# RWKV-7 attention with a hardswish FFN: b and k turned by VectorE from second loads by quarters, and the last features of y copied by GpSimd

## The chip, the cores and the metric

One core of a Trainium2 chip runs the whole kernel. Its engines work side by side, each through its own list of instructions in order: TensorE (PE in the profile) multiplies matrices and, by a multiplication with the identity, transposes them; VectorE (DVE), ScalarE (ACT) and GpSimd (POOL) work on elements; SyncE (SP) issues transfers here. PEld is PE's loading of the stationary operand. Semaphores tie the lists together. The metric is the device time of one execution in microseconds; lower is better. A comparison uses the median of several executions.

## The reference

There are 4 batches, 8 heads, 768 steps and a head dimension of 40, all in fp32. For each batch and head a state of 40x40 runs through the steps, and the output of a step is read before the state is updated:

```python
for t in range(S):
    y[:, :, t] = np.einsum('bhd,bhde->bhe', rt, state)
    Sa = np.einsum('bhde,bhe->bhd', state, at)
    state_decay = state * wt[:, :, None, :] - np.einsum('bhd,bhe->bhde', Sa, bt)
    state = state_decay + np.einsum('bhd,bhe->bhde', vt, kt)
```

The 8 x 40 = 320 outputs of a step are then one token of an FFN over 3072 tokens, 320 to 2048 to 320:

```python
h = x @ w_in
g = h * np.clip(h + 3.0, 0.0, 6.0) / 6.0
out = g @ w_out
```

## The kernel before

The recurrence is computed in blocks of 64 steps. A **unit** is one block of one pair of batches, so there are 24 units (0 to 23), and four units are a group (128 steps of all batches). Steps lie on the partitions in the loads; for the products, features have to lie there, so the inputs are transposed.

Work of a unit comes in named stages of two kinds. `prepare(i)` is ahead of the recurrence: W and gam (running products of the decay w: gam, and its inverse rgam), A, B, K (the inputs turned so that features lie on the partitions, and multiplied by gam or rgam: `at`, `bt`, `kt`), F and E (masked products of these), factor (rgam turned back, from which GpSimd makes KBt, k and b with steps on the partitions, L725) and EV (E times v, L752). `step(i)` goes with the recurrence: fade, RT, VT, R, C, S, U, UT, rS, H, ysn (the outputs y), then `move` and `move2`, which bring the 320 features of y from the tile `yg` into the layout that the FFN reads, `xt`, three pieces of 128, 128 and 64 features. The triangular systems of a group are solved together by `invert`, a chain of some sixty dependent VectorE operations (L804, L810) with copies around it.

The order of the instructions on each engine is written out in the code; no scheduler moves them. From unit 8 on `a_block(m)` emits the stages, a block at a time. A unit begins every three blocks from unit 8 to 12, and every four from unit 13 on. `together` issues the PE products of all stages of a block in the order of PRODUCTS, and then what reads their results in the order of RESULTS; products of a block share PSUM tiles of two banks (`pair`) where they fit. Between the blocks `feed` puts pieces of the FFN (`expand`, L1171 and `short`, L1184, the first product; L1193 and L1194 the activation; `contract`, L1219, the second product) and of the inversion. `short` takes the 64 last features; beside a product that uses only half of the array it goes in fours of 64x64.

How the inputs are turned: from unit 8 on, b is turned by `turn_halves` (L516, eight PE transposes into PSUM) and k by `turn_pairs` (L506, four PE transposes). a, and r from unit 4 on, are already turned by VectorE: `turn_blocks` (L524 to L531) uses VectorE's transpose of 32x32 blocks, and for this the tile has to be loaded by quarters (`fetch`, L478: four transfers, 32 partitions each, of 80 or 48 features a head pair). A tile that is loaded so holds the values in an order that only this transpose reads; GpSimd's KBt needs b and k as they come in the plain loads (L490, two transfers).

SP issues all of this: loads, `xt` moves (`move`, L1111, four transfers; `move2`, L1116, four more of 32 features x 128 tokens each), outputs (L1243) and the weights' pieces at the start (L343). It is one queue in order: a transfer whose tile is still in use holds back all that stand behind it. `fetch` for the next unit is called in the stage that has read the tile: a's in A, b's and k's in factor behind KBt, v's in K (that of the unit itself). The weights arrive as eight pieces of w_in and those of w_out in the first 150 us, and ScalarE and VectorE convert each (L393 to L403, a factor; the raw pieces lie in tiles that are used for something else later). FEATURES says which features of the model go on which partitions of which of the three pieces, and so how w_in is loaded: two transfers a piece.

The tiles `xt` come from a ring of six, which also lends places to the first sums of the FFN (`part`, L1228).

Of the kernel before, what the change touches and what calls it, by code (L numbers as in the profile page):

```python
# [17 lines left out]
P = 128  # L18
BL = 64
HB = BL // 2  # L20
L = 32
# [10 lines left out]
def kernel(  # L32
# [179 lines left out]
    area = const.tile([P, EDGE + 3 * H * BL], F32, name="area")  # L212
# [30 lines left out]
    tinv = const.tile([P, NH, BL], F32, name="tinv")  # L243


    state, last_dec = [], []
    for p in range(NP):
# [12 lines left out]
        [(0, 0, 2 * D), (2 * D, 4 * D, D + 8)],  # L260
        [(0, 2 * D, 2 * D), (2 * D, 6 * D, D + 8)],
        [(0, 5 * D + 8, L), (L, 7 * D + 8, L)],
# [188 lines left out]
    def fetch(name, i, engine=None):  # L451

        if i is None or i >= NK:
            return
        x, crossed = {"W": (w, 0), "A": (a, 0), "B": (b, 0), "K": (k, 0), "R": (r, 1),
                      "V": (v, 1)}[name]
        if name == "V":
            t = values[i % AHEAD]
        else:
            t = placed.get((name, i))  # L460
            if (name, i) == ("R", 1):
                t = others["K"]
            if (name, i) == ("W", NU + 1):
                t = values[NU]
            t = t if t is not None else (others if i < 2 * NU and i % 2 and name != "R" else inputs)[name]
        g, p = names[i]
        engines = engine or nc.sync
        if name == "R" and i >= NU or name == "A" and i >= 2 * NU:
            y = x[2 * p:2 * p + 2, :, g * BL:(g + 1) * BL, :]
            n = 2 if name == "R" else 1  # L470
            y = y.rearrange("q (k s j) t e -> s j (q k) (t e)", s=2, j=n).rearrange(
                "s j k (l e) -> s j l k e", e=2 * D)
            for s in range(2):
                for c in range(0, D, L):
                    z = s * SLOT + c
                    to = rooms[name][z:z + L].rearrange("l (j k e) -> l j k e", j=n, e=2 * D)
                    for j in range(n):
                        nc.sync.dma_start(out=to[:, j, :, 0:2 * D - c], in_=y[s, j, :, :, c:])  # L478
            data[i][name + "N"] = t
            return  # L480
        for q in range(2):
            engine = engines[q] if isinstance(engines, tuple) else engines
            y = x[2 * p + q, :, g * BL:(g + 1) * BL, :]
            rows = slice(q * BL, (q + 1) * BL)
            if crossed:
                for s in range(2):
                    engine.dma_start(out=t[rows, 4 * s:4 * s + 4, 0:D],
                                     in_=y[s::2].rearrange("h t e -> t h e"))
            else:
                engine.dma_start(out=t[rows, :, 0:D], in_=y.rearrange("h t e -> t h e"))  # L490
        data[i][name + "N"] = t
# [32 lines left out]
    def turn_blocks(to, name):  # L524

        x = rooms[name].rearrange("p (j k y e) -> p j k y e", j=2, y=2, e=D)[:, :, :, :, 0:L]
        if name == "A":
            nc.vector.transpose(out=to[:].rearrange("p r (q t y) -> p q r y t", q=2, y=2), in_=x)
            return
# [32 lines left out]
    def begun_beside():  # L562

        begin = -(-(SCAN + 1) // 16) * 16
        for n, name in enumerate("KB"):
            x = area[:, begin + n * H * JOIN:begin + (n + 1) * H * JOIN]
            nc.gpsimd.memset(x, 0.0)
            beside[name] = x.rearrange("p (h t) -> p h t", h=H)
        beside["E"] = grp.tile([P, H, BL], F32, name="E", tag="U", bufs=1)
        nc.gpsimd.memset(beside["E"][:], 0.0)  # L570
        for name in "rgam", "RT":
# [10 lines left out]
    def prepare(i, F):  # L582
        n, o = i % NU, data[i]
        halves = i >= 2 * NU
# [68 lines left out]
        def b_stage():  # L653
            x = turn_in(o["BN"], halves)
            yield PE
            bt = o["bt"] = turned("bt")
            for y, z, g in zip(parts_of(bt, halves), x, parts_of(o["rg"], halves)):
# [74 lines left out]
        def k_stage():  # L732
            x = turn_pairs(o["KN"])
            yield PE
            kt = o["kt"] = turned("kt")
            nc.vector.tensor_tensor(out=kt[:], in0=x[:], in1=o["rg"][:], op=ALU.mult)
# [24 lines left out]
        return {"W": w_stage, "gam": gam_stage, "A": a_stage, "B": b_stage, "F": f_by_32 if i < 2 * NU else f_by_64,  # L761
# [121 lines left out]
    def step(i):  # L883
# [216 lines left out]
        def s_move():  # L1100
            xt = m["xt"] = ffn.tile([P, 3, P], F32, name="xt", bufs=6)
            yg = m["yg"]
            moves = m["moves"] = [(xt[0:D, 0:2], yg[0:D, 0:2, :]),
                     (xt[D:2 * D, 0:2], yg[SLOT:SLOT + D, 0:2, :]),
                     (xt[2 * D:3 * D, 0:2], yg[0:D, 2:4, :]),
                     (xt[3 * D:P, 0:2], yg[SLOT:SLOT + 8, 2:4, :])]
            for c in range(4):
                moves.append((xt[c * L:(c + 1) * L, 2],
                              yg[SLOT + 8:SLOT + D, 2 + c % 2, :]))
            for dst, src in moves[:4]:  # L1110
# [3 lines left out]
        def s_move2():  # L1114
            for dst, src in m["moves"][4:]:
                nc.sync.dma_start(out=dst, in_=src)  # L1116
# [94 lines left out]
    def contract(i, r, gts):  # L1211
# [13 lines left out]
        if r == 0:  # L1225
            sums[i] = op
            if split:
                part = ffn.tile([P, 3 * P], F32, name="part", tag="xt", bufs=6)[:, 0:DM]  # L1228
# [219 lines left out]
    for _ in range(18):  # L1448
# [16 lines left out]
    RESULTS = ["ysn", "W", "VT", "EV", "R", "S", "C", "A", "B", "move", "move2", "open",  # L1465
               "U", "UT", "rS", "F", "K", "fade", "H", "E", "factor", "RT", "gam"]
# [42 lines left out]
    def a_block(m):  # L1509

        if coming and begins[coming[0]] == m:
            u = coming.popleft()
            close = coming and begins[coming[0]] < m + BLOCKS
            ahead[u, m] = prepared(u), CLOSE_STAGES if close else AHEAD_STAGES
# [29 lines left out]
    for i in range(NU, NK):  # L1544
        spread[0] = i >= 2 * NU - 1
        for j in range(BLOCKS):
# [20 lines left out]
            m += 1  # L1567
    for _ in range(2):
# [36 lines left out]
```

## Time and profile before

| what | us |
|---|---|
| median of 3 executions (range) | 773.98 (773.76 to 776.44) |
| the profiled execution, its own time | 772.7 |
| its span in the trace | 771.0 |
| PE busy (share of the span) | 710.8 (92%) |
| VectorE busy | 508.8 (66%) |
| ScalarE busy | 310.4 (40%) |
| GpSimd busy | 150.8 (20%) |
| first and second FFN product, PE busy | 229.2 and 230.4 |
| two lines of the inversion, VectorE busy | 64.1 and 63.0 |
| bytes moved | 48.43 MB in 175999 packets |

The second part of the profile page shows the busy share in 40 slices of 19 us, in tenths:

```profile
PE   4635888999899989999999999999999999999997
DVE  8899968588557799556798456898436982333210
PEclk7956799999999999999999999999999999999999
```

It is read from left to right: in the first five slices (some 95 us) weights are still arriving and PE is half empty; then PE is full but for a slice or two; VectorE swings with the inversions of the groups. PEclk is the clock that PE was granted. In the groups of instructions, each row has line, engine, operation, tiles, shape and count, then busy time in all and mean ns of one, then idle time ahead of them and what ended it. In a timeline, each row has the start, the length and the instructions.

### The profile page before, as it was taken

The page shows a single profiled execution, that of the slowest core. Times are in us where ns is not written, and L with a number is a line of the kernel's source. Part 1 is how long each engine was busy: PE and PEld are TensorE (multiplying, and loading weights), DVE is VectorE, ACT ScalarE, POOL GpSimd, SP SyncE. Part 2 cuts the span into 40 slices and gives each one's busy share as a digit, 9 for nine tenths or more (in the row PEclk, how much of TensorE's full clock was granted, in tenths as well). Part 3 has the DMA queues.
Part 4 walks back from the last instruction along what each step waited for, and adds up shares of the span by engine and source line. Part 5 has one row for each costly group of instructions (what it writes and reads, how often), then busy time and mean ns, then how long its engine had stood idle before and what let it go on. Part 6 is the DMA issues. An engine that isn't in the chain of part 4 may idle for free.

```text
span 771.0 us, 33034 instructions
## 1 busy us (share of the span) xinstructions
PE 710.8 (92%) x14568; PEld 603.1 (78%) x14568; DVE 508.8 (66%) x1027; ACT 310.4 (40%) x644; POOL 150.8 (20%) x303
## 2 busy tenths in 40 slices
PE   4635888999899989999999999999999999999997
PEld 3534777778779778888888888888888888888885
DVE  8899968588557799556798456898436982333210
ACT  2377865232553324552434453234444224322211
POOL 7403210321322211212112121203112010000000
PEclk7956799999999999999999999999999999999999
DMA  9685563420334322233322223313331110110000
GB/s 124 119 179 150 114 170 57 79 43 18 64 65 84 70 55 48 52 71 60 64 52 55 53 62 63 69 37 60 57 72 42 25 24 23 35 35 12 14 16 19
DMA packets 175999, 48.43 MB, mean 63 GB/s; under 512 B 159216, under 2 KB 174576, under 8 KB 175856
## 3 DMA queue, kind: packets, MB, share of 16 engines
q1 hardware_dynamic: 171552, 45.58, 29.7%
q8 instruction: 115, 1.88, 1.0%
q10 hardware_dynamic: 4304, 0.74, 0.7%
q14 instruction: 28, 0.23, 0.1%
HBM read 37.62 MB, written 3.93 MB: 54 GB/s over the span
## 4 chain that ended last, share of the span: by engine, by line
PE 77%; DVE 8%; SPq 5%; issue 3%; DMA 3%; ACT 3%; POOL 0%; DVEq 0%; ACTq 0%; POOLq 0%
PE o L1219 25%; PE h L1171 24%; PE pair L554 4%; PE pair L1064 4%; SPq L490 3%; PE h L1184 2%; PE one L506 2%; PE pair L968 2%; PE pair L927 1%; DVE prod L804 1%; PE pair L1007 1%; PE pair L516 1%; PE pair L752 1%; DVE x L810 1%; PE pair L1023 1%
## 5 line engine op out<-in xcount | busy, mean ns | idle before, releaser
L1171 PE MATMUL h<-xt,win 128*128 128x128 f32 (+1 forms) x2000 | 229.2, 282 | 3.0 <-DVE gt L1194 3.0
L1219 PE MATMUL o<-wout,gt 128*128 128x320 f32 x768 | 230.4, 443 | 0.0
L1171 PEld LDWEIGHTS h<-xt,win 128*128 128x128 f32 (+1 forms) x2000 | 212.9, 193 | 17.5 <-issue 3.1
L1219 PEld LDWEIGHTS o<-wout,gt 128*128 128x128 f32 x768 | 138.6, 190 | 50.3 <-issue 0.2
L1193 ACT ACTIVATE gt<-h,three 128x512 f32<-128x512 f32 x96 | 62.6, 686 | 110.3 <-PE h L1171 88.0
L1194 DVE SCALAR_TENSOR_TENSOR gt<-gt,h 128x512 f32<-128x512 f32 x96 | 61.8, 679 | 62.4 <-ACT gt L1193 62.3
L578 DVE COPY_PREDICATED area<-mask,pair 128x512 f32<-128x512 int32 x56 | 40.5, 726 | 55.2 <-PE pair L554 36.7
L804 DVE TENSOR_TENSOR prod<-x 128x30 f32<-128x30 f32 (+9 forms) x180 | 64.1, 356 | 8.9 <-POOL x L789 3.3
L810 DVE TENSOR_TENSOR x<-x,prod 128x30 f32<-128x30 f32 (+9 forms) x180 | 63.0, 350 | 5.5
L725 POOL TENSOR_TENSOR KBt<-K,rgt 128x320 f32<-128x320 f32 x22 | 19.1, 866 | 142.2 <-ACT rgt L714 134.2
L1071 DVE TENSOR_TENSOR ys<-pair,ys 128x512 f32<-128x512 f32 x20 | 13.8, 690 | 40.5 <-PE pair L1064 40.5
L993 POOL COPY area<-V 128x320 f32<-128x320 f32 x20 | 9.1, 454 | 149.6 <-DVE area L645 53.7
L757 ACT ACTIVATE EV<-pair 64x320 f32<-64x320 f32 x44 | 19.0, 432 | 39.2 <-PE pair L752 38.9
L1064 PE MATMUL pair<-area,KBt 64*64 64x104 f32 x1280 | 32.4, 250 | 0.0
L1237 ACT ACTIVATE ob<-o 128x320 f32<-128x320 f32 x22 | 9.6, 435 | 56.6 <-PE o L1219 35.2
L603 DVE TENSOR_TENSOR_SCAN prods<-area,start 128x528 f32<-128x528 f32 x24 | 29.9, 1250 | 3.4 <-ACT area L599 3.3
L632 POOL COPY gam<-prods 128x256 f32<-128x256 f32 x24 | 12.7, 531 | 99.1 <-DVE prods L603 99.1
L614 DVE TENSOR_TENSOR_SCAN area<-area,start 128x528 f32<-128x528 f32 x24 | 30.6, 1276 | 0.8
L1064 PEld LDWEIGHTS pair<-area,KBt 64*64 64x64 f32 x1280 | 29.9, 133 | 1.5 <-issue 1.4
L872 ACT ACTIVATE tinv<-pair 32x256 f32<-32x256 f32 x48 | 18.0, 375 | 31.9 <-PE pair L862 31.3
L931 DVE TENSOR_TENSOR RR<-pair,EV 128x320 f32<-128x320 f32 x22 | 10.7, 485 | 20.9 <-PE pair L554 13.6
L633 POOL COPY rgam<-prods 128x256 f32<-128x256 f32 x22 | 23.9, 1084 | 0.0
(289 smaller groups left out, 1078.5 us busy)
## 6 DMA issues: line engine op xcount, KB each, us to landing
V<-in_v_dram SPq DMA_DIRECT2D x96, 40.0 KB
out_dram<-ob SPq DMA_DIRECT2D x47, 80.0 KB
R<-in_r_dram SPq DMA_DIRECT2D x92, 40.0 KB
B<-in_b_dram SPq DMA_DIRECT2D x42, 80.0 KB
K<-in_k_dram SPq DMA_DIRECT2D x42, 80.0 KB
W<-in_w_dram SPq DMA_DIRECT2D x37, 80.0 KB
A<-in_a_dram SPq DMA_DIRECT2D x37, 80.0 KB
xt<-yg SPq DMA_DIRECT2D x72, 40.0 KB
```

What stands on the lines that cost most here:

```text
L554: nc.tensor.matmul(out=o[i][half(q), n ^ (2 * q * placed), :], lhsT=lhs[half(i, D), n ^ (2 * q * swap), half(q)], rhs=rhs[half(i, D), n, h ...
L578: nc.vector.copy_predicated(out=x[:].rearrange("p (i h) t -> p i h t", i=2), mask=mask8, data=o[2])
L603: nc.vector.tensor_tensor_scan(out=prods[:].rearrange("p r m i -> p (r m i)"), data0=wm[:, 0:SCAN], data1=start[:], initial=0.0, op0=ALU.m ...
L614: nc.vector.tensor_tensor_scan(out=back, data0=back, data1=start[:], initial=0.0, op0=ALU.mult, op1=ALU.add)
L633: nc.gpsimd.tensor_copy(rv[:, :, 0:HB], o["prods"][:, :, 0, 0:HB][:, :, ::-1])
L804: nc.vector.tensor_tensor(out=pv, in0=_ap(x[:], (i + 1) * L + i, [[L, n], [0, i]]), in1=_ap(x[:], i * L, [[0, n], [1, i]]), op=ALU.mult,)
L810: nc.vector.tensor_tensor(out=rest, in0=rest, in1=pv, op=ALU.add)
L1064: nc.tensor.matmul(out=both[q][half(s), pr, :], lhsT=o[name][half(q), h * D:h * D + SLOT], rhs=beside[name][half(q), 4 * rs + 2 * (s ^ (q ...
L1171: nc.tensor.matmul(out=hp[c][:, i, :], lhsT=lhsT, rhs=rhs, start=(begun[c] == 0), stop=(begun[c] == 3 * NQ - 1))
L1193: nc.scalar.activation(out=gt[:], in_=hp[c][:], func=AF.Relu, bias=three[:], scale=1.0)
L1194: nc.vector.scalar_tensor_tensor(out=gt[:], in0=gt[:], scalar=6.0, in1=hp[c][:], op0=ALU.min, op1=ALU.mult)
L1219: nc.tensor.matmul(out=op[:], lhsT=gts[c][:, n, :], rhs=wout[:, c * HJ + r * NQ + n, :], start=((split or r == 0) and c == 0 and n == 0), ...
```

## The change

1. From unit 9 on (`by_quarters`), b and k are loaded a second time, by quarters, into two more tiles, Bq (in `area`, made longer) and Kq (in the tile that now holds the `xt` places). `turn_blocks` turns them with VectorE's transpose straight into `bt` and `kt`, which are then multiplied by rgam in place. The PE transposes of these units, 8 for b and 4 for k, are gone. The plain loads stay, for KBt. The stages carry names of their own (Bq, Kq) in the order of a block, so that they are not counted among the PE products or given PSUM; R and C come to share a `pair` tile by this. Each of the two tiles gets a GpSimd memset once. The quarter load of a unit stands on SP's queue behind the transpose of the unit before.
2. `move2` of units 4 to 23 is four GpSimd copies of 32x128 instead of four transfers on SP. For this the last 64 features of the FFN's input are the first 32 of a slot, not the last 32, and FEATURES is laid out anew: w_in's pieces need three transfers each instead of two.
3. The ring of six `xt` tiles becomes one tile with six fixed places, four of them used by turns.

```diff
-    area = const.tile([P, EDGE + 3 * H * BL], F32, name="area")
+    PLACE = -(-(SCAN + 1) // 16) * 16
+    TAIL = PLACE + 2 * H * (BL + D)
+    area = const.tile([P, TAIL + 2 * H * D], F32, name="area")
...
+    XT = 6
+    xts = ffn.tile([P, XT, 3 * P], F32, name="xts")
...
     FEATURES = [
-        [(0, 0, 2 * D), (2 * D, 4 * D, D + 8)],
-        [(0, 2 * D, 2 * D), (2 * D, 6 * D, D + 8)],
-        [(0, 5 * D + 8, L), (L, 7 * D + 8, L)],
+        [(0, 0, 2 * D), (2 * D, 4 * D, D), (3 * D, 5 * D + L, D - L)],
+        [(0, 2 * D, 2 * D), (2 * D, 6 * D, D), (3 * D, 7 * D + L, D - L)],
+        [(0, 5 * D, L), (L, 7 * D, L)],
     ]
...
         x, crossed = {"W": (w, 0), "A": (a, 0), "B": (b, 0), "K": (k, 0), "R": (r, 1),
-                      "V": (v, 1)}[name]
+                      "V": (v, 1), "Bq": (b, 0), "Kq": (k, 0)}[name]
...
-            t = placed.get((name, i))
+            t = rooms.get(name) if name[1:] else placed.get((name, i))
...
-        if name == "R" and i >= NU or name == "A" and i >= 2 * NU:
+        if name == "R" and i >= NU or name == "A" and i >= 2 * NU or name[1:]:
...
-        if name == "A":
+        if name != "R":
             nc.vector.transpose(out=to[:].rearrange("p r (q t y) -> p q r y t", q=2, y=2), in_=x)
...
+        rooms["Bq"] = area[:, TAIL:]
+        nc.gpsimd.memset(rooms["Bq"], 0.0)
+        fetch("Bq", 2 * NU + 1)
...
-        halves = i >= 2 * NU
+        halves, by_quarters = i >= 2 * NU, i > 2 * NU
...
         def b_stage():
-            x = turn_in(o["BN"], halves)
+            x = [None] if by_quarters else turn_in(o["BN"], halves)
             yield PE
             bt = o["bt"] = turned("bt")
+            if by_quarters:
+                x = parts_of(bt, halves)
+                turn_blocks(bt, "Bq")
+                fetch("Bq", following(i))
             for y, z, g in zip(parts_of(bt, halves), x, parts_of(o["rg"], halves)):
                 nc.vector.tensor_tensor(out=y, in0=z, in1=g, op=ALU.mult)
...
         def k_stage():
-            x = turn_pairs(o["KN"])
+            x = None if by_quarters else turn_pairs(o["KN"])
             yield PE
             kt = o["kt"] = turned("kt")
+            if by_quarters:
+                x = kt
+                turn_blocks(kt, "Kq")
+                fetch("Kq", following(i))
             nc.vector.tensor_tensor(out=kt[:], in0=x[:], in1=o["rg"][:], op=ALU.mult)
             if i > 2 * NU:
                 fetch("V", i)
...
         def s_move():
-            xt = m["xt"] = ffn.tile([P, 3, P], F32, name="xt", bufs=6)
+            xt = m["xt"] = xts[:, i % NU].rearrange("p (c t) -> p c t", t=P)
             yg = m["yg"]
-            moves = m["moves"] = [(xt[0:D, 0:2], yg[0:D, 0:2, :]),
+            moves = [(xt[0:D, 0:2], yg[0:D, 0:2, :]),
                      (xt[D:2 * D, 0:2], yg[SLOT:SLOT + D, 0:2, :]),
                      (xt[2 * D:3 * D, 0:2], yg[0:D, 2:4, :]),
-                     (xt[3 * D:P, 0:2], yg[SLOT:SLOT + 8, 2:4, :])]
-            for c in range(4):
-                moves.append((xt[c * L:(c + 1) * L, 2],
-                              yg[SLOT + 8:SLOT + D, 2 + c % 2, :]))
-            for dst, src in moves[:4]:
+                     (xt[3 * D:P, 0:2], yg[SLOT + L:SLOT + D, 2:4, :])]
+            for dst, src in moves:
                 nc.sync.dma_start(out=dst, in_=src)
...
         def s_move2():
-            for dst, src in m["moves"][4:]:
-                nc.sync.dma_start(out=dst, in_=src)
+            for c in range(4):
+                dst, src = m["xt"][c * L:(c + 1) * L, 2], m["yg"][SLOT:SLOT + L, 2 + c % 2]
+                if i < NU:
+                    nc.sync.dma_start(out=dst, in_=src)
+                else:
+                    nc.gpsimd.tensor_copy(dst, src)
...
-                part = ffn.tile([P, 3 * P], F32, name="part", tag="xt", bufs=6)[:, 0:DM]
+                part = xts[:, XT - SPLIT + i, 0:DM]
...
-    RESULTS = ["ysn", "W", "VT", "EV", "R", "S", "C", "A", "B", "move", "move2", "open",
-               "U", "UT", "rS", "F", "K", "fade", "H", "E", "factor", "RT", "gam"]
+    RESULTS = ["ysn", "W", "VT", "EV", "R", "S", "C", "A", "B", "Bq", "move", "move2", "open",
+               "U", "UT", "rS", "F", "K", "Kq", "fade", "H", "E", "factor", "RT", "gam"]
...
-            ahead[u, m] = prepared(u), CLOSE_STAGES if close else AHEAD_STAGES
+            order = CLOSE_STAGES if close else AHEAD_STAGES
+            ahead[u, m] = prepared(u), [[x + "q" if x in "BK" and u > 2 * NU else x for x in y] for y in order]
...
             m += 1
+            if m == 2:
+                assert not any(x in sums for x in range(SPLIT))
+                rooms["Kq"] = _ap(xts[:], (XT - SPLIT) * 3 * P, [[1, 2 * H * D]])
+                nc.gpsimd.memset(rooms["Kq"], 0.0)
+                fetch("Kq", 2 * NU + 1)
```

More of the change, by code (lines that the diff above doesn't have):

```diff
@@ L562, in begun_beside @@
     def begun_beside():
-        begin = -(-(SCAN + 1) // 16) * 16
         for n, name in enumerate("KB"):
-            x = area[:, begin + n * H * JOIN:begin + (n + 1) * H * JOIN]
+            x = area[:, PLACE + n * H * JOIN:PLACE + (n + 1) * H * JOIN]
             nc.gpsimd.memset(x, 0.0)
@@ L759, in ev_stage @@
             o["EV"] = EV
-        return {"W": w_stage, "gam": gam_stage, "A": a_stage, "B": b_stage, "F": f_by_32 if i < 2 * NU else f_by_64,
+        return {"W": w_stage, "gam": gam_stage, "A": a_stage, "B": b_stage, "Bq": b_stage, "Kq": k_stage, "F": f_by_32 if i < 2 * NU else f_by_64,
                 "factor": factor_stage, "K": k_stage, "E": e_stage, "EV": ev_stage}
```

## The prediction

> **What bounds the kernel now.** I read the page's busy line and its chain first, then the stretches, then the matmul engine's waits, then the queue of loads.
>
> ```profile
> PE 710.8 (92%) x14568; PEld 603.1 (78%) x14568; DVE 508.8 (66%) x1027; ACT 310.4 (40%) x644; POOL 150.8 (20%) x303
> PE 77%; DVE 8%; SPq 5%; issue 3%; DMA 3%; ACT 3%; POOL 0%; DVEq 0%; ACTq 0%; POOLq 0%
> ```
>
> The chain is TensorE (PE) for 77%. Where is PE not full? The busy times by stretch (columns: stretch and length, then busy us and instructions of PE, weight loads, VectorE, ScalarE, GpSimd; granted clock, share of the DMA engines, GB/s):
>
> ```profile
> 195.00:264.00 69.00, 66.68 (x1626) 55.49 (x1628) 43.74 (x81) 31.48 (x78) 17.18 (x34) 1.00 0.38 73
> 264.00:281.00 17.00, 14.06 (x246) 11.39 (x240) 15.86 (x40) 2.74 (x6) 3.67 (x10) 0.99 0.32 58
> 281.00:304.00 23.00, 23.00 (x381) 19.57 (x380) 21.76 (x51) 8.19 (x18) 2.87 (x6) 0.94 0.24 47
> 304.00:381.40 77.40, 77.40 (x1799) 66.57 (x1795) 48.65 (x96) 35.48 (x82) 18.25 (x34) 1.00 0.32 63
> 381.40:415.50 34.10, 34.10 (x588) 28.96 (x584) 31.61 (x69) 11.93 (x23) 6.74 (x11) 1.00 0.24 48
> ```
>
> From 281 us on PE has no idle time, so there a removed PE instruction is time gained one for one. From 264 to 304 VectorE is busy 37.6 of 40 us: the inversion of group three sets the pace. All of PE's waits for another engine from 216 us to the end are these:
>
> ```profile
> PE pair L752 <- DVE area L645: 1.9, 1, 1.9
> PE pair L554 <- DVE E L578: 0.7, 1, 0.7
> PE h L1171 <- DVE gt L1194: 0.3, 1, 0.3
> ```
>
> The other resource near its end is SP, the one in-order queue that issues every load and move. In its timeline it issues without a gap from 195.2 to 273 us, while units 8 to 12 start every three blocks; each group below starts as the one before it ends (start, length, line):
>
> ```profile
> 244.50 2.99 SPq L487 DMA_DIRECT2D V<-in_v_dram  x4
> ...
> 250.39 3.68 SPq L1111 DMA_DIRECT2D xt<-yg  x4
> 254.12 2.47 SPq L1116 DMA_DIRECT2D xt<-yg  x4
> 256.69 2.16 SPq L490 DMA_DIRECT2D W<-in_w_dram  x2
> 258.95 2.05 SPq L478 DMA_DIRECT2D A<-in_a_dram  x4
> ```
>
> Later it has gaps: from 300 to 400 us it issues for 85, and after that it stands idle for about 10 us in every third unit or so.
>
> **What leaves PE.** Units 9 to 23 lose eight transposes of b (L516) and four of k (L506). The groups say what they are, the rows beside them what they cost in the pipeline:
>
> ```profile
> L506 PE MATMUL one<-ident,K 128*128 128x128 f32 x76 | 11.5, 274 | 0.0
> L516 PE MATMUL pair<-ident,B 64*128 64x64 f32 x128 | 7.1, 230 | 0.0
> L528 DVE STREAM_TRANSPOSE at<-A 128x512 f32<-128x512 f32 x16 | 11.0, 689 | 0.0
> ```
> ```profile
> 447.63 0.41 PE L516 MATMUL pair<-ident,B 64*128 64x64 f32 x8
> 447.97 0.68 PE L927 MATMUL pair<-state,at 40*64 40x40 f32 x32
> ```
>
> Starts count, since matmuls overlap: b's eight hold PE from 447.63 to 447.97, 0.34 us (0.40 in two other units), k's four from 427.16 to 427.69, 0.53. That is 0.9 us for each unit. Units 13 to 23 lie in the full stretch: 11 x 0.9 = 9.9 us off. The list of instructions also shows the FFN's 64-wide products going in fours in some 11 more places, 0.92 us apart rather than 1.00: 0.8 off. Sum: -10.7.
>
> **Unit 12 (264 to 304 us).** Its 0.9 goes too. Without b's PSUM tile, R and C share one, and the wait of 1.9 and of 0.7 above come from such buffers and the order around them. After the 1.9 us wait eight L1171 matmuls took 2.07 us, against 1.16 elsewhere, and the granted clock of the stretch was 0.94; so up to 0.9 + 2.6 + 1.3 = 4.8 off. But VectorE has 2.4 us left in these 40, and gets four operations more (below). Between 0 and -4; I take -2, the middle.
>
> **VectorE.** Each unit adds two transposes of 128x512. An independent one starts the next after 0.61 us, one whose result is used at once after 0.80 (A's, 424.63 to 425.42): 1.6 us per unit, 24 in all. The multiplies stay (L658 682 ns with PSUM, L650 692 from SBUF). Outside the inversions VectorE has a third of its time free. In the inversions of the steady part (381.4 to 415.5: 31.61 of 34.10) 2.5 us are left, less the 0.9 that PE gains; the FFN's wait of 0.3 on gt says that the slack is small. Between 0 and +3 (three inversions of about 1 us); I take +1.
>
> The rgam copy on GpSimd (L633) took 0.40 us alone at 233.12 and 1.37 at 197.02, with a scan beside it, so the two engines do hold each other up. The Trainium skill, page "SBUF — State Buffer", section "🔬 SBUF: two separate sides", makes this a lock: a VectorE operation with two SBUF inputs and a GpSimd operation that reads SBUF shut each other out for a whole instruction. By that rule the two multiplies, which now read both inputs from SBUF, could each wait for a copy of 0.45 us: an estimate of 2.7 us more over the six of three inversions, and no gain left; L650, which reads both from SBUF already, shows no such lengthening, so my sum leaves it out.
>
> **GpSimd.** 80 copies of 32x128 replace 80 moves of 32x128. By L993's 128x320 (454 ns) as the upper and L912's 128x8 (189 ns at its shortest) as the lower row, 0.2 to 0.45 us each, up to 1.8 per unit. GpSimd is busy 6.74 of 34 us there, and KBt, which stands behind the copies on its queue, waits 10 us for rgt at 244 anyway: nothing, and up to 0.5 us per unit if that cover were gone.
>
> **SP, the steady part.** Per unit eight quarter loads come and four moves go. A's four quarters take 1.8 to 3.1 us, mostly 2.2: +4.4; the moves (L1116) 2.5 to 3.8, 2.8 in the mean: net +1.6 us. From 438.1 to 488.7 SP has 5.0 us of gaps in two units, in front of b's load, which waits for KBt on GpSimd. So it fits, with about 1 us per unit left: 0. V's load now stands behind both quarter groups, and V is needed by L752 some 3 us after it lands; at the narrowest (457.17 + 2.73, landing near 462, used at 466.3) about 1.5 are left after the change.
>
> **SP, the ramp.** Here there are no gaps. Ahead of V for unit 10, issued at 244.50, SP must now also issue quarters of b and k for units 9, 10 and 11: six groups x 2.3 = 13.8 us, less one group of moves (3.2) and a gap of 0.5: 10 us late. That V is used here:
>
> ```profile
> 252.58 0.68 PE L752 MATMUL pair<-V,E 64*64 64x40 f32 x32
> ```
>
> It landed about 2 us after its last issue, near 249.4, so there is 3 us of slack; PE meanwhile gets some 2 us shorter or has already lost them to earlier loads. 10 - 3 - 1 = +6, between 3 (quarters at 1.8) and 8. W of unit 12 is late by 7 in the same queue and is covered by this stall. After an idle stretch PE restarts slower (0.9 us on eight matmuls above): +1.5 for a longer one. Moves of xt late in this stretch, and two memsets of 128x640 on GpSimd (0.6 us by L570's 128x512 at 0.53): +0.7. Sum +8.2.
>
> **SP, the start.** Each of eight pieces of w_in now takes three transfers instead of two. SP is gapless from 0.8 to 58 us, at about 0.62 us per issue there; three or four of the extra ones are ahead of the transfer for which ScalarE waits 3.5 us at 55.45, on the chain. Between 0 (the bytes are the same) and 3.5; I take 2.
>
> **Sum**: -10.7 - 2 + 1 + 8.2 + 2 = -1.5. The profiled execution took 772.7 (span 771.0 and 1.7 around), 1.3 under the median of 773.98; so 771.2 for such an execution and 772.5 as a median.
>
> **Rivals.**
> Faster: the quarters come free. They are asked for a unit ahead, so V's place might hide as the page's idle SP suggests. Then 15 x 0.9 + 0.8 + 2 leave with the start's 0 to 2 back and a ramp cost of at most 3: 759 to 766, about 763. For it: from 281 on nothing but PE binds. Against: the gapless SP from 195 to 273.
> Slower: SP becomes the bound beyond the ramp. It decides where a quarter group takes over about 2.7 us (net 2.6 per unit, against gaps of 2.5): some are that long (3.08 at 427.68). At 3.1 us, 3.4 - 2.5 = 0.9 per unit and 11 units, +10, and +4 in the ramp: about 786; at 2.8, 778 to 780. Against: the long gaps of about 10 us every third unit.
> VectorE as the bound: the whole 1.6 us per unit in four inversions, two units each, +13 at worst, 4 likely, gives 776; it lies inside my range.
> That the change doesn't do what it says is excluded: the listing shows the 180 PE transposes gone.
>
> **How the numbers follow.** This kernel's runs lie 0.35% apart, so 0.5%, 3.9 us, is what can be told from no change: 770.1 to 777.9. Near balance, 767 to 778: 0.48, and of it 0.10 below 770.1. Faster rival 0.27. Slower rival 0.25, 778 to 786. Faster 0.37, same 0.38, slower 0.25. The range leaves out the lower end of the faster rival and the upper of the slower: 762 to 781.
>
> **What would show it.** PE's matmuls 180 fewer and its busy time about 14 lower; STREAM_TRANSPOSE of bt and kt near 690 ns; the waits on L645 and E gone; a new PE wait on DMA V at L752 of 3 to 8 us near 255; the gap in front of b's load shrunk to 1 us from 430 on; ScalarE's 3.5 us at 55 grown to about 5.5. Wrong it would be by a quarter group far from 2.3 us, by a wait in every unit rather than one, or by VectorE late in each inversion.

## The result, and the profile after

The changed kernel took 779.53 us (median of 17, 775.14 to 785.35); the kernel before, beside it, 773.98 (17, 771.90 to 779.99). The ratio is 1.0074, 95% interval 1.0056 to 1.0091: slower by 0.7%, where -1.5 us was forecast. The profiled execution took 782.8 us (span 781.1), 3.3 over its median; that of before stood 1.3 under its own. So the two traces lie 10.1 us apart and the medians 5.5, and some of what the traces show is the luck of two executions.

The page's busy line and chain of the changed kernel:

```profile
PE 710.7 (91%) x14484; PEld 600.6 (77%) x14484; DVE 530.4 (68%) x1057; ACT 309.6 (40%) x644; POOL 176.8 (23%) x385
PE 57%; DVE 21%; SPq 8%; issue 5%; DMA 4%; ACT 2%; POOL 1%; DVEq 0%; POOLq 0%; ACTq 0%
```

TensorE has 84 matmuls fewer: 180 transposes less, and 96 more since `short` goes in fours in twelve places (800 records for 608). Its busy time is the same to 0.1 us, where 14 less was forecast: part of what was saved was spent at half clock, as will be seen. The chain was 77% TensorE and is 57%; VectorE went from 8 to 21%, SP from 5 to 8%. The stretches at the same times as before:

```profile
195.00:264.00 69.00, 61.12 (x1492) 50.15 (x1491) 46.15 (x85) 31.80 (x75) 23.60 (x48) 0.95 0.42 81
264.00:281.00 17.00, 17.00 (x270) 13.22 (x265) 9.26 (x16) 6.16 (x15) 3.18 (x7) 0.89 0.43 86
281.00:304.00 23.00, 17.76 (x336) 14.27 (x327) 21.49 (x54) 6.60 (x15) 3.98 (x11) 0.96 0.36 72
304.00:381.40 77.40, 77.10 (x1763) 66.29 (x1763) 54.01 (x103) 33.96 (x77) 21.14 (x40) 0.97 0.38 74
381.40:415.50 34.10, 34.07 (x593) 28.73 (x593) 30.09 (x67) 12.09 (x27) 8.26 (x19) 1.00 0.38 77
```

From 195 to 264 us TensorE has lost 5.6 us of busy time, from 281 to 304 another 5.2, and the granted clock of four stretches is below 1. The five longest of its waits from 190 us to the end:

```profile
PE h L1186 <- DVE x L824: 4.1, 1, 4.1
PE pair L766 <- DMA V<-in_v_dram: 3.7, 4, 2.4
PE pair L853 <- DVE state L1087: 1.7, 2, 0.9
PE pair L876 <- DVE area L651: 1.5, 1, 1.5
PE pair L695 <- DVE bt L668: 1.4, 3, 0.8
```

The old waits of 1.9 (L752 on L645) and 0.7 us are gone as forecast, and V at L766 (L752 before) is the new one. The place of each can be read from TensorE's timeline:

```profile
261.25 0.41 PE L766 MATMUL pair<-V,E 64*64 64x40 f32 x2 [2.44 <-DMA V<-in_v_dram]
262.54 0.44 PE L766 MATMUL pair<-V,E 64*64 64x40 f32 x4 [0.89 <-DMA V<-in_v_dram]
263.14 1.07 PE L766 MATMUL pair<-V,E 64*64 64x40 f32 x26 [0.16 <-DMA V<-in_v_dram]
264.15 2.50 PE L1234 MATMUL o<-wout,gt 128*128 128x320 f32 x4
...
302.74 7.80 PE L1186 MATMUL h<-xts,win 128*128 128x128 f32 x48 [4.13 <-DVE x L824]
```

After the wait of 3.5 us in all, four L1234 matmuls take 2.50 us; the same four took 1.34 before (at 253.19). SP's timeline shows why V came late:

```profile
254.12 2.64 SPq L482 DMA_DIRECT2D area<-in_b_dram  x4
256.85 2.04 SPq L482 DMA_DIRECT2D xts<-in_k_dram  x4
258.94 2.59 SPq L491 DMA_DIRECT2D V<-in_v_dram  x4
```

V of unit 10 is issued at 258.94, 14.4 us later than before, with the quarters of b (`area`) and k (`xts`) for unit 11 just ahead. TensorE and VectorE were 6.6 us late by then; the queue accounts for the other 7.8.

Following the same instruction in both traces gives the lag of the changed kernel over the run, here at the first scan of a unit (L603, L609) and, in the last column, as the difference of the spans. The rows of the experiments are told below. Times are those of the kernel before; all in us.

| kernel | 128 | 195 | 268 | 307 | 496 | 580 | end |
|---|---|---|---|---|---|---|---|
| the change | 5.8 | 5.4 | 12.2 | 15.1 | 12.3 | 10.8 | 10.1 |
| copies alone | -0.2 | -0.8 | 0.8 | 1.0 | 1.0 | 1.1 | 0.6 |
| weights split alone | 2.3 | 1.0 | 1.0 | 1.5 | 0.5 | 0.5 | 0.1 |
| quarters from 13 | 1.1 | 1.8 | 3.5 | 3.8 | 3.4 | 2.7 | 1.4 |
| quarters on ScalarE's queue | 2.5 | 3.4 | 12.6 | 14.5 | 11.4 | 10.2 | 9.6 |
| loads alone | 4.6 | 3.8 | 10.8 | 11.0 | 11.5 | 11.4 | 10.6 |
| turns alone | 0.2 | 0.6 | 0.7 | 2.6 | -1.0 | -2.7 | -3.5 |
| k only | 3.9 | 3.1 | 5.9 | 7.1 | 4.7 | 5.0 | 4.0 |
| V first | 4.1 | 4.2 | 9.2 | 11.1 | 7.5 | 5.9 | 5.1 |
| quarters alone | 2.2 | 1.5 | 9.7 | 12.0 | 17.1 | 16.6 | 17.4 |
| V first, from 13 | 5.5 | 6.5 | 8.1 | 8.3 | 9.5 | 8.9 | 7.6 |
| k, V first, from 13 | 1.7 | 2.0 | 2.0 | 2.5 | 0.2 | -0.5 | -1.5 |
| b turned sooner | 5.5 | 5.0 | 6.7 | 6.8 | 5.9 | 4.6 | 3.6 |

The first row has three parts: 5.4 us before 195 us, 9.7 more up to 307 (6.8 by 268 and 2.9 behind it), and then 5.0 given back.

### The profile page after: what moved, and what is told of

The parts are those of the page before. It is cut to its first block, busy times and chain, and to the rows that moved or that the text cites. A ratio compares the mean times of both kernels' runs of the same rounds, so it can differ in the third digit from the quotient of the medians.

```text
span 781.1 us, 33020 instructions
## 1 busy us (share of the span) xinstructions
PE 710.7 (91%) x14484; PEld 600.6 (77%) x14484; DVE 530.4 (68%) x1057; ACT 309.6 (40%) x644; POOL 176.8 (23%) x385
## 4 chain that ended last, share of the span: by engine, by line
PE 57%; DVE 21%; SPq 8%; issue 5%; DMA 4%; ACT 2%; POOL 1%; DVEq 0%; POOLq 0%; ACTq 0%
PE h L1186 19%; PE o L1234 18%; DVE x L824 4%; DVE prod L818 4%; PE pair L558 4%; SPq L482 3%; PE pair L1078 3%; PE h L1199 3%; SPq L494 2%; SPq L491 2%; DVE gt L1209 2%; DVE prods L609 1%; DMA R<-in_r_dram 1%; DVE area L584 1%; PE one L510 1%
## 5 line engine op out<-in xcount | busy, mean ns | idle before, releaser
L1186 PE MATMUL h<-xts,win 128*128 128x128 f32 (+1 forms) x1904 | 227.0, 286 | 9.7 <-DVE x L824 4.1
L1234 PE MATMUL o<-wout,gt 128*128 128x320 f32 x768 | 230.7, 443 | 0.0
L1186 PEld LDWEIGHTS h<-xts,win 128*128 128x128 f32 (+1 forms) x1904 | 211.1, 196 | 24.0 <-DVE x L824 4.6
L1234 PEld LDWEIGHTS o<-wout,gt 128*128 128x128 f32 x768 | 138.7, 190 | 50.5 <-issue 0.4
L1209 DVE SCALAR_TENSOR_TENSOR gt<-gt,h 128x512 f32<-128x512 f32 x96 | 61.7, 678 | 59.4 <-ACT gt L1208 58.0
L1131 POOL COPY xts<-yg 32x128 f32<-32x128 f32 x80 | 43.9, 549 | 156.0 <-DVE yg L1088 148.5
L609 DVE TENSOR_TENSOR_SCAN prods<-area,start 128x528 f32<-128x528 f32 x24 | 30.0, 1253 | 4.1 <-ACT area L605 4.0
L620 DVE TENSOR_TENSOR_SCAN area<-area,start 128x528 f32<-128x528 f32 x24 | 30.6, 1275 | 0.8
L1199 PE MATMUL h<-xts,win 64*64 64x128 f32 x800 | 27.6, 275 | 0.0
L1199 PEld LDWEIGHTS h<-xts,win 64*64 64x64 f32 x800 | 21.6, 132 | 3.8 <-issue 2.9
L840 POOL COPY tinv<-tb 32x1024 f32<-32x1024 f32 x10 | 10.3, 1034 | 61.9 <-DVE tb L827 48.7
```

The source lines that it names most:

```text
L609: nc.vector.tensor_tensor_scan(out=prods[:].rearrange("p r m i -> p (r m i)"), data0=wm[:, 0:SCAN], data1=start[:], initial=0.0, op0=ALU.m ...
L1131: nc.gpsimd.tensor_copy(dst, src)
L1186: nc.tensor.matmul(out=hp[c][:, i, :], lhsT=lhsT, rhs=rhs, start=(begun[c] == 0), stop=(begun[c] == 3 * NQ - 1))
L1199: nc.tensor.matmul(out=hp[c][half(z), i, :], lhsT=y[:, half(z)], rhs=xt[half(c), 2, :], start=(begun[c] == 0), stop=(begun[c] == 3 * NQ - 1))
L1209: nc.vector.scalar_tensor_tensor(out=gt[:], in0=gt[:], scalar=6.0, in1=hp[c][:], op0=ALU.min, op1=ALU.mult)
L1234: nc.tensor.matmul(out=op[:], lhsT=gts[c][:, n, :], rhs=wout[:, c * HJ + r * NQ + n, :], start=((split or r == 0) and c == 0 and n == 0), ...
```

## The experiments

Three causes were open: the extra weight transfers at the start, the quarter loads' place in SP's queue, and VectorE's added work. Each kernel is the changed one with an edit, unless said otherwise; medians are of 6 to 12 executions, ratios against the kernel before on the same chip (773.70 to 774.61 us there). Medians of two experiments can come from two chips.

**Copies alone.**

```diff
-        halves, by_quarters = i >= 2 * NU, i > 2 * NU
+        halves, by_quarters = i >= 2 * NU, False
...
-        fetch("Bq", 2 * NU + 1)
...
-                fetch("Kq", 2 * NU + 1)
```

> The second and third part of the change alone: GpSimd copies for move2, w_in in three transfers a piece, fixed xt places; b and k are turned by TensorE as before and there are no second loads. Theory (SP's queue decides: extra weight transfers at the start, quarter loads in the ramp): the lag behind the kernel before is +2 at 47 us and +3 to +5 at 130 us, then it stays or shrinks by 0 to 2 in the ramp, since SP has 3 us less to issue per unit; 775 to 779 us in all, ratio 1.002 to 1.006. Rival (the 80 GpSimd copies hold VectorE up): the lag grows in every unit from 4 on, by 0.3 or more, 781 us and over.

Measured 774.35 us, ratio 1.0007 (0.9991 to 1.0023): no difference, and under both sums. The GpSimd copies cost nothing, and the weights' transfers neither; the old 1.9 us wait is still there. In the mean a copy takes longer than I had bounded:

```profile
L1131 POOL COPY xts<-yg 32x128 f32<-32x128 f32 x80 | 43.9, 549 | 156.0 <-DVE yg L1088 148.5
L1131 POOL COPY xts<-yg x80: 279/288/1227, 225.9 to 742.0; 32x128 f32<-32x128 f32 x80
```

This is their group in the page of the changed kernel, and below it the shortest, the median and the longest. The mean hides two kinds: 57 copies took 0.28 to 0.40 us, inside my bounds, and 23 took 0.78 to 1.23. Of these, 22 start while a scan of VectorE runs (L609 or L620, some 1.25 us) and end 0.07 to 0.10 us after it. GpSimd waits most of the time, so this cost nothing.

**Weights split alone**, the kernel before with one edit.

```diff
-        [(0, 0, 2 * D), (2 * D, 4 * D, D + 8)],
-        [(0, 2 * D, 2 * D), (2 * D, 6 * D, D + 8)],
+        [(0, 0, 2 * D), (2 * D, 4 * D, D), (3 * D, 5 * D, 8)],
+        [(0, 2 * D, 2 * D), (2 * D, 6 * D, D), (3 * D, 7 * D, 8)],
```

> The kernel before with one edit: each of the eight w_in pieces that came in two transfers per half comes in three, same bytes, same layout. Theory: R of the first unit lands 1.9 us later and the lag at 130 us is +2 to +5.5, all of which lasts to the end: 776 to 779.5 us. Rival (the lag at 130 us in the one profile of the changed kernel is the chance of the clock in a stretch where TensorE is half idle): +0.5 to +2, 774.5 to 776 us.

Measured 773.97 us, ratio 1.0002 (0.9984 to 1.0020). The theory missed; the time lies just under the rival's 774.5. In the trace R of the first unit did come later, and 2.3 us of lag stood at 128 us; by 195 it was 1.0.

**Quarters from unit 13 on**, so without the ramp.

```diff
-        halves, by_quarters = i >= 2 * NU, i > 2 * NU
+        halves, by_quarters = i >= 2 * NU, i >= 13
...
-                turn_blocks(bt, "Bq")
-                fetch("Bq", following(i))
+                turn_blocks(bt, "Bq")
+            if i >= 12:
+                fetch("Bq", following(i))
```

(k in the same way.)

> As the changed kernel, but b and k are turned by quarters from unit 13 on only, the first quarter loads asked for by unit 12. Theory: no wait of L766 on V near 255 us and no halved clock after it, so the lag stays near +5 through 195 to 264 us; the steady part gives back 5 as it does in the changed kernel; 772 to 776 us, 4 to 7 faster than the changed kernel. Rival (VectorE's added transposes in the inversions are the loss): the wait of L1186 on the inversion near 300 us and the steps of 0.5 to 0.9 later remain, 777 to 780 us.

Measured 774.02 us, ratio 1.0006 (0.9982 to 1.0031); 5.5 faster than the change. So the loss belongs to units 9 to 12, and the eleven steady units with all the saving in them gain nothing that can be told from the copies alone. The lag falls from 3.8 at 307 us to 1.4 at the end, 2.4 us, where 9.7 net was forecast. TensorE's waits from 300 us on:

```profile
PE pair L854 <- DVE state L1088: 1.7, 2, 0.9
PE pair L767 <- DMA V<-in_v_dram: 1.6, 1, 1.6
PE pair L695 <- issue: 1.1, 2, 0.9
PE pair L695 <- DVE bt L668: 0.3, 1, 0.3
```

The kernel before has no wait after 300 us in this list; here they add up to 5.0, with 0.3 of it under "issue" at L558. Part is V again, in one unit; the rest are products that wait for VectorE's results (L695 is the product of bt and at), and some whose releaser the profile does not show.

**Quarters on ScalarE's queue** (units 9 to 13).

```diff
-                        nc.sync.dma_start(out=to[:, j, :, 0:2 * D - c], in_=y[s, j, :, :, c:])
+                        (nc.scalar if name[1:] and i <= 13 else nc.sync).dma_start(
+                            out=to[:, j, :, 0:2 * D - c], in_=y[s, j, :, :, c:])
```

> As the changed kernel, but the quarter loads of b and k for units 9 to 13 are issued on ScalarE's queue; SP issues the rest. Theory (place in SP's queue): V of unit 10 is issued some 10 us sooner, L766 waits under 1 us there, the lag at 266 us falls from +12 to +6 or +7, and the total to 771 to 776 us unless ScalarE's queue is held up by the waits. Rival (the transfers themselves are slow, the DMA engines being shared): V still lands late and the total stays at 778 to 781.

Measured 785.49 us, ratio 1.0156 (1.0118 to 1.0194): slower still, a miss of both sums. TensorE no longer waits on V anywhere from 195 to 310 us, as the theory says; but a group holds ScalarE for 2 to 3 us, and TensorE waits for ScalarE instead, or for VectorE's gt, which reads what ScalarE's L1209 writes (the first fence has two issues from ScalarE's timeline, the second TensorE's longest waits from 195 to 310 us).

```profile
265.19 3.12 ACTq L482 DMA_DIRECT2D area<-in_b_dram  x4
271.00 3.05 ACTq L482 DMA_DIRECT2D xts<-in_k_dram  x4
```

```profile
PE h L1187 <- DVE gt L1210: 5.3, 2, 3.8
PE one L964 <- ACT area L606: 3.4, 1, 3.4
```

**Loads alone, turns alone**: the two halves of the quarters taken apart. In the first, b and k are turned by TensorE and the quarter loads are issued for nothing; in the second, only unit 9's quarters are loaded and later units turn the same data.

```diff
# loads alone
-        halves, by_quarters = i >= 2 * NU, i > 2 * NU
+        halves, by_quarters = i >= 2 * NU, False
...
-                turn_blocks(bt, "Bq")
-                fetch("Bq", following(i))
+                turn_blocks(bt, "Bq")
+            if i > 2 * NU:
+                fetch("Bq", following(i))
... (k in the same way)
# turns alone
-                fetch("Bq", following(i))
...
-                fetch("Kq", following(i))
```

> The changed kernel with b and k of units 9 to 23 turned by TensorE from the plain loads, as before; the quarter loads are issued where the change has them, but nothing reads them. Beside the copies alone (774.35) it adds the 120 quarter loads and nothing else. Theory (place in SP's queue): V of unit 10 late, L766 waits 3 to 4 us near 258 us with a halved clock behind it, some 1.6 us on V in one later unit: 780 to 783 us. Rival (VectorE's transposes are the loss): 774 to 776 us.

> The changed kernel with the first quarter loads only: VectorE turns what unit 9 loaded in every unit from 9 on, so the output is wrong from the second unit turned so; all instructions of TensorE, VectorE, ScalarE and GpSimd stay, and 112 transfers are gone from SP. Theory (SP's queue): no wait on V; TensorE's 0.9 us per unit come through but for about 1 to 2 us in each inversion: 766 to 770 us. Rival (VectorE): the wait of L1186 near 300 us and of L695 and L853 on VectorE's results remain, 774 to 779 us.

Loads alone: 785.96 us, ratio 1.0137 (1.0108 to 1.0167). Turns alone: 769.51 us, ratio 0.9932 (0.9908 to 0.9956). Against the kernel before on their own chips, copies alone stand at +0.7 us, loads alone at +11.4 and turns alone at -5.1. Over the copies the loads thus cost 10.7 and the turns bring 5.8, and the parts add up: 0.7 + 10.7 - 5.8 = 5.6, against 5.5 for the change. So the loads are the whole loss, and what TensorE's and VectorE's exchange of work brings is a gain of about 6, not the 13 that the transposes held. Loads alone lie above the theory's 780 to 783, and another transfer than V is late there, the plain load of b, which TensorE's transposes need:

```profile
PE pair L520 <- DMA B<-in_b_dram: 3.6, 3, 2.3
```

The waits of the turns alone have no transfer among them, and the longest name VectorE (three of them below); those on gt lie between 243 and 302 us:

```profile
PE h L1184 <- DVE gt L1207: 5.4, 4, 2.4
PE pair L851 <- DVE state L1085: 2.5, 3, 0.9
PE pair L694 <- DVE bt L667: 1.3, 3, 0.7
```

Of the 10.6 us of lag of the loads alone, 3.8 stand already at 195 us, when the first quarter load has only just been issued. That part is looked at below.

**k only.**

```diff
-            x = [None] if by_quarters else turn_in(o["BN"], halves)
+            x = turn_in(o["BN"], halves)
...
-            if by_quarters:
-                x = parts_of(bt, halves)
-                turn_blocks(bt, "Bq")
-                fetch("Bq", following(i))
```

> As the changed kernel for k alone; b is turned by TensorE as before, with no second load of it. TensorE saves 0.53 us in 15 units, 8 us; SP issues 2.2 us more and 2.8 us less (copies) per unit; ahead of V of unit 10 there are three quarter groups rather than six. Theory: V of unit 10 about 3 us late, which its slack covers; VectorE adds 0.8 us per unit and the tight b product (L695) is as before: 767 to 771 us. Rival (VectorE's transposes cost more than TensorE's save whatever the queue): 774 us and over.

Measured 775.62 us, ratio 1.0008 (0.9989 to 1.0026): a miss upwards, to the rival's number. From 195 to 307 us the lag still grows by 4.0, with TensorE's wait on b's plain load (2.9 us in four) in place of V: with half the groups the queue is still late. After 307 it falls by 3.1.

**V first.**

```diff
-                fetch("Bq", following(i))
...
-                fetch("Kq", following(i))
...
             if i > 2 * NU:
                 fetch("V", i)
+                fetch("Bq", following(i))
+                fetch("Kq", following(i))
```

> The changed kernel with one order altered: the quarter loads of b and k for the next unit are both issued behind this unit's V, in the K stage, instead of ahead of it. Theory: V of unit 10 has four quarter groups ahead of it rather than six and lands 5 us sooner; L766 waits about 1 us instead of 3.5, no wait on V later: 774 to 777 us. Rival (VectorE): 778 to 781 us.

Measured 775.74 us, ratio 1.0011 (0.9993 to 1.0029): 3.8 faster than the change by the order of transfers alone (4.4 if each is taken against the kernel before beside it). V's wait falls from 3.7 us to 1.4.

**Quarters alone**: without the copies, move2 by SP and the old layout.

```diff
...
-                if i < NU:
+                if True:
                     nc.sync.dma_start(out=dst, in_=src)
```

> The first part of the change alone: b and k of units 9 to 23 by quarters and VectorE, but move2 stays four transfers on SP, w_in comes in two transfers a piece and the layout is the old one. Theory (SP's queue): another group of moves (3.2 us) stands ahead of V in the ramp, and in the steady part SP has 2.8 us more per unit than in the changed kernel, over its 24 us; V and the plain loads late in several units: 784 to 792 us. Rival (the copies are a cost of their own and not a relief): 776 to 780 us.

Measured 791.38 us, ratio 1.0238 (1.0211 to 1.0265). The copies are worth 11.9 us beside the quarters and nothing without them (774.35): they free a queue that only the quarters fill. Here SP is late beyond the ramp too, the slower rival of the prediction: five of the nine waits on V, 4.7 us of 7.8, lie behind 307 us.

```profile
PE pair L766 <- DMA V<-in_v_dram: 7.8, 9, 1.7
PE h L1186 <- DMA xts<-yg: 4.0, 1, 4.0
```

**V first, from 13**, both edits; and the same **for k alone**.

> Both edits that took time off: quarters from unit 13 on, and issued behind V. Theory: no wait on V or B anywhere, the 1.6 us on V near 466 us of the kernel with quarters from 13 on goes; what is left is TensorE's 0.9 us in 11 units less the steps in three inversions (0.9 to 3 us each): 769 to 773 us. Rival (VectorE's cost in the inversions equals TensorE's saving): 773 to 775 us.

> The same for k alone: k by quarters from unit 13 on, behind V; b by TensorE. TensorE saves 0.53 us in 11 units, 5.8 us; VectorE adds 0.8 us a unit. Theory: 769 to 772 us, since the b product that waited on VectorE keeps its old way; rival (each transpose on VectorE costs in the inversions what it saves): 773 to 775 us.

The first took 774.57 us, ratio 1.0012 (0.9990 to 1.0033): the rival's number. With no wait on a transfer left, eleven units' transposes taken from TensorE bring nothing: the lag is 8.3 at 307 us and 8.9 at 580. The longest waits from 300 us on:

```profile
PE pair L693 <- issue: 3.1, 3, 1.4
PE pair L853 <- DVE state L1087: 1.7, 2, 0.9
PE pair L853 <- issue: 0.8, 1, 0.8
PE pair L693 <- DVE bt L666: 0.6, 2, 0.3
```

L693 is the product of bt and at, and VectorE now does four operations in a row for these two (from 347.63 to 350.53 us, 2.9) where three took 2.1 (from 424.63 in the kernel before). The next experiment takes L693's waits for this chain. Two lines of VectorE's timeline and two of TensorE's show that the long ones are something else:

```profile
349.03 0.70 DVE L532 STREAM_TRANSPOSE bt<-area 128x512 f32<-128x512 f32 x1
349.84 0.69 DVE L666 TENSOR_TENSOR bt<-bt,rgam 128x512 f32<-128x512 f32 x1
351.73 0.52 PE L693 MATMUL pair<-bt,at 40*64 40x64 f32 x22
353.06 0.44 PE L693 MATMUL pair<-bt,at 40*64 40x64 f32 x10 [0.81 <-issue]
```

The product begins 1.2 us after bt is done, and waits after 22 of its 32 matmuls. The other two of these three waits, at 327.29 and 575.41, stand within the product in the same way. VectorE's lateness by name is 2.3 us here: on bt in two units, on the state in two. The 4.2 us under "issue" (3.1, 0.8 and 0.3 more in one place) have no releaser in the profile; more on them in the last section. With k alone the median is 772.66 us, ratio 0.9985 (0.9968 to 1.0001), between the two sums and just short of a difference.

**b turned sooner**: V first, from 13, and VectorE turns b behind the copies of gam, a block earlier.

```diff
+            if by_quarters:
+                o["bt"] = turned("bt")
+                turn_blocks(o["bt"], "Bq")
             yield from ()
...
-            bt = o["bt"] = turned("bt")
+            bt = o["bt"] = o["bt"] if by_quarters else turned("bt")
             if by_quarters:
                 x = parts_of(bt, halves)
-                turn_blocks(bt, "Bq")
```

> The kernel with quarters from unit 13 on, issued behind V, and one edit more: VectorE turns b a block earlier, behind the copies of gam, and only multiplies it in the B stage. The same operations, the same count. Theory (what ate the steady saving is that the product of b and a now waits for four VectorE operations in a row instead of three): the waits of the b product, 0.3 to 1.4 us in five or so units, go, and with them 4 to 5 us: 769 to 772 us. Rival (VectorE's added time counts, wherever it stands): 773 to 775.5 us.

Measured 772.15 us, ratio 0.9973 (0.9950 to 0.9995): between the two sums, and by 0.3% faster than the kernel before. The same operations a block earlier brought 2.4 us over V first, from 13; the intervals of the two ratios still touch. The waits from 300 us on:

```profile
PE pair L695 <- issue: 2.4, 3, 1.2
PE h L1188 <- DVE gt L1211: 1.3, 2, 0.6
```

6.5 us of them have become 3.7; those on the state (L853) and on bt by name, 2.3 us, are gone, so VectorE's order counted, as far as this noise lets one tell. The product's own long waits are still there: at 325.58 us it waits 1.2 us, while bt was finished at about 322.1.

## Why the prediction was wrong

The sign of the sum was wrong, by 7 us: -1.5 was forecast, +5.5 came. That the time lies inside the stated range is luck: that part of the range belonged to the slower rival, SP late beyond the ramp, and this is not what happened. Two steps failed: unit 12, which was to gain 2 us and lost 2.9, and the steady part, which was to gain 9.7 net and gained 5.0.

**Unit 12** (-2, between 0 and -4) failed in its sign. The prediction says itself that the inversion of group three sets the pace from 264 to 304 us, and yet counts TensorE's saving there. In the table, the five kernels that turn both b and k on VectorE in units 9 to 12 lag 1.9 to 2.9 us more at 307 us than at 268 (turns alone, which issues no quarter loads behind unit 9's, 1.9); k only lags 1.2 more, and the seven that turn neither there 0.1 to 0.5. The transposes arrive in VectorE's chain at their full length. This is the operation of the inversion behind the multiply of bt, in the kernel before and in the changed one:

```profile
282.33 0.39 DVE L804 TENSOR_TENSOR prod<-x 128x234 f32<-128x234 f32 x1
295.43 0.40 DVE L818 TENSOR_TENSOR prod<-x 128x234 f32<-128x234 f32 x1
```

It is 13.1 us late; ahead of at and bt the inversion was 12.3 late, and behind kt it is 13.9. The waits of 1.9 and 0.7 us went, as forecast, and TensorE came back to a lag of 6.9 (its L982 at 293.18, L968 at 286.32 before). But at 302.74 it waited 4.13 us and then ran 6.8 us at half clock, and stood at 15.1. The profile puts this wait down to an operation of the inversion. It was the moves of xt: TensorE passes its last semaphore for them at 302.63 us in the trace, and the fourth move lands at 302.61. SP's lines before and after:

```profile
281.05 1.80 SPq L478 DMA_DIRECT2D A<-in_a_dram  x4
282.89 3.09 SPq L1111 DMA_DIRECT2D xt<-yg  x4
```

```profile
293.32 3.01 SPq L482 DMA_DIRECT2D A<-in_a_dram  x4
296.43 1.88 SPq L482 DMA_DIRECT2D area<-in_b_dram  x4
298.36 3.07 SPq L1122 DMA_DIRECT2D xts<-yg  x4
```

The moves stand behind a's quarters, which wait until VectorE has turned the a before (3.4 us at 293.32), and now behind b's too: 15.5 us later than before. So TensorE could not keep what it gained while VectorE stayed 12 to 14 us late. This is the "xt late" that was priced at a few tenths.

The other steps:

- *What leaves PE* (-10.7) held: in the lags each unit passes with 0.4 us less for b and 0.4 to 0.5 for k, 9.2 us in eleven units where 9.9 was forecast. Failed is that a removed instruction is time gained one for one: 4.2 of the 9.2 are handed back behind 307 us. By name TensorE waits there for VectorE (the state 1.7 us, bt 0.6) and for "issue" (0.4); the rest shows no wait.
- *VectorE* (+1, 0 to 3): these 2.3 us lie within its range, since two of the inversions do cost some 0.9 us each at L853. It is in unit 12, where the sum set nothing down for it, that VectorE cost most. Over all units, turns alone bring 5.8 us of the 13 transposed.
- *SP, the ramp* (+8.2) held, on the place that was named: 6.8 by 268 us. Loads alone lag 7.0 there, turns alone 0.1, so it is the loads. V was 7.8 us later than its surroundings rather than 10; TensorE waited 3.5 us and then ran at half clock, together +5.6 against +6 and +1.5.
- *SP, the start* (+2): 0, between -1.2 and +1.5 by the weights split alone. TensorE's first product on R began 1.9 us later, and ScalarE's wait at 55 us, which was to grow from 3.5 to 5.5, took 3.8.
- *SP, the steady part* (0) holds with the copies and only just: no wait on V in the changed kernel after 300 us, 1.6 us in one unit of the kernel from 13 on. The quarters alone show the other side of that edge: +11.9.
- *GpSimd* (0) held in cost. The rule of the Trainium skill, page "SBUF — State Buffer", section "🔬 SBUF: two separate sides", that a VectorE operation with two SBUF inputs and a reading GpSimd operation shut each other out, is not seen in VectorE's times: the multiply of bt from two SBUF inputs took 692 ns over 15 units with 80 copies about, and 682 with PSUM. It is seen in GpSimd's: the 22 copies that start within a scan, which reads two SBUF tiles, end with it. The one that began second waited.
- Of the rivals, neither of the two named by direction was right alone. The faster one missed that loads matter, the slower one needed the steady part. VectorE as the bound, set at 776, had the mechanism of unit 12.

From this one trace the parts behind 195 us add up to 6.8 + 2.9 - 5.0 = 4.7. Ahead of it stand 5.4 us, of which 0.6 belongs to the kernel: GpSimd clears Bq for 0.63 us at 198.74, ahead of an operation that VectorE waits for, and the lag goes from 4.8 to 5.4. That makes 5.3, against 5.5 by the medians.

What stays open are the other 4.8 us of the traces' 10.1. The same early stretch gave between -0.8 and 6.5 us in the thirteen traces. The clock, which changes between half and full several times before 130 us, differs among them. Most of it looks like the chance of one execution: the three traces that lag most at 195 us (V first, from 13, the change, b turned sooner: 6.5, 5.4, 5.0) are of executions 5.7, 3.3 and 4.3 us above their medians, while those of turns alone and copies alone (0.6, -0.8) lie 0.2 and 1.1 below. Loads alone and ScalarE's queue do not fit (3.8 and 3.4, and 2.5 and 3.2 below), so some of it may belong to the kernel.

## What to carry to other kernels

Price a move between engines by the chain that the moved work joins, not by the share of time that its new engine has free. Where the new engine sets the pace (here VectorE in unit 12) the moved work cost its full length and the old engine's gain was worth nothing; where the old one did, about half of the gain came through. A queue that issues without a gap is a bound like an engine: find what stands behind the new transfers, put the urgent ones first, and begin where there are gaps. Relief for such a queue (here the copies) is worth nothing by itself and much beside what fills it, so measure both parts together and apart.

## What the runs showed of the hardware

A short idle time of TensorE can cost more than itself. Stretches at half clock begin in or behind its waits: 261 to 268 us after 3.5 us on V, 302 to 309 after 4.13; and the kernel before had one behind its wait of 1.91 us. The stretches of the changed kernel, then of the kernel before (granted clock third from the end):

```profile
261.00:268.00 7.00, 5.70 (x76) 3.98 (x76) 1.15 (x2) 0.86 (x2) 0.00 (x0) 0.51 0.44 84
...
302.00:309.00 7.00, 6.26 (x30) 6.29 (x31) 6.52 (x18) 0.00 (x0) 0.00 (x0) 0.51 0.20 41
```

```profile
280.60:284.00 3.40, 3.40 (x42) 3.12 (x42) 3.19 (x7) 1.97 (x4) 1.26 (x4) 0.51 0.39 81
```

Each such stretch lasts 3.4 or 6.8 us and nearly doubles what runs in it (2.50 us for 1.34 above): up to 1.7 or 3.4 us on top of the wait. The Trainium skill, page "TensorE: Matmul & The Clock Gate", Part 1 ("The HAM clock gate"), has the clock halved after an idle window of about 3.4 us; the lengths here agree with that window, but a wait of 1.9 us, much less than a window, was at times enough. Nine traces have this wait, and seven show a stretch of 3.4 us at half clock behind it; weights split alone and k, V first, from 13 show none, nor does turns alone behind a wait of 2.39 us.

A group of four transfers held ScalarE for up to 3.1 us when ScalarE issued it, about what it takes SP.

TensorE's waits under "issue" go with the loading of instructions. In the traces of all fourteen kernels, from 190 to 700 us, 22 of its waits over 0.25 us have no releaser; ahead of each, a transfer of 16 KB of instructions ended 1.3 to 1.5 us before TensorE went on. Of the 141 waits with a releaser 7 have one there. So it is likely that TensorE was waiting for its own code, 4.2 us in V first, from 13; no run varies it.
